# Five pairs of 512 tokens from the ninth unit on, two of their output tiles computed from g kept in the place of w_in, and attention ahead of them in even steps

## The chip, the cores and the metric

The program runs on one core of a Trainium2 chip. The metric is device time in microseconds (us) of one execution; lower is better. A core has these engines, each with an instruction stream of its own that runs in order: TensorE (PE in the profile; its weight loads are listed as PEld), VectorE (DVE), ScalarE (ACT), GpSimd (POOL) and SyncE (SP), which here issues nearly all DMA transfers. They wait for one another by semaphores. PE reads its operands from the on-chip memory SBUF and writes to the accumulators in PSUM.

## What is computed

Linear attention with positive random features (8 batches, 8 heads, 576 tokens, head dimension 64, 128 features), and behind it a layer of two matrix products on all 4608 tokens of 512 values:

```python
def phi(x):
    proj = np.einsum('bhsd,md->bhsm', x, omega)
    h = proj - np.sum(x * x, axis=-1, keepdims=True) / 2.0
    h = h - np.max(h, axis=-1, keepdims=True)
    return np.exp(h) / np.sqrt(m)
q_p, k_p = (phi(q_s), phi(k_s))
kv = np.einsum('bhsm,bhsd->bhmd', k_p, v)
num = np.einsum('bhsm,bhmd->bhsd', q_p, kv)
den = np.einsum('bhsm,bhm->bhs', q_p, np.sum(k_p, axis=2))[..., None] + 1e-06
x = num / den          # 4608 x 512 behind the transpose of the heads
h = x @ w_in           # 512 x 2048
g = h - np.tanh(h)
out = g @ w_out        # 2048 x 512
```

## The kernel before

**Precision.** Operands of the large products are split into a high and a low part in the type fp32r (`xh`, `xl`; `gh`, `gl`; two halves of each weight tile), and three products high*high, high*low, low*high are summed.

**Units and steps.** Tokens go through the second layer in units of 256 (`TC`), 18 in all, and its 2048 inner columns in 16 tiles `f` of 128. Units 0 and 1 run together, 512 columns wide, while the weights are still being decoded (`decode`, L435 to L451, from 1 MB tiles `raw` that DMA brings). From unit 2 on a unit has 8 steps `s`, each of two tiles f. In a step `ffn_h` (L468) makes 24 matmuls of 128x256 (2 f, 4 parts c of x's 512 values, 3 products) into one PSUM tile h, then ACT takes the tanh (L472), DVE subtracts it from h (L473), ACT casts to gh (L474) and DVE makes gl (L475). `ffn_out` (L486 to L488) adds the 12 products of the step before, 128x512 each, to the two output tiles `po0` and `po1` of the unit. A weight tile `wt[f]` holds, for both parts, 512 values of w_in and 512 of w_out.

**Attention.** Its work from batch 2 on and for units 3 to 17 runs between the steps, in generators: `k_unit(b, c)` for batch b and head pair c, `q_unit(ch, c)` for unit ch. There are four c to each. A q loads `qf`, splits it into `qx`, makes features, sums the denominator with `zb`, scales, transposes (`pt`), splits into `qh` and `ql`, multiplies with `kvw` (`pn`), adds two halves into `xs` (L397 to L400) and splits that into `xh` and `xl` (L406, L407). A table `start` says at which beat each generator begins; a step has two beats, and at each beat every living generator goes on to its next `yield`:

```python
for ch in range(3, NCH):
    for c in range(NC):
        k = 28 + 4 * c if ch == 3 else 42 + 4 * c if ch == 4 else 16 * (ch - 1) - 6 + 4 * c
        start.setdefault(k, []).append(("q", ch, c))
for b in range(2, B):
    for c in range(NC):
        k = 31 + 5 * c if b == 2 else 16 * (need[b] - 1) - 25 + 8 * c
```

Unit 2 begins at beat 32, unit ch at 16*ch. Ahead of the first step of a unit the loop runs generators on until the x of this unit is complete (`xdone`).

**Order.** A scheduler puts the instructions of each engine into their final order from the order of the code and from what they depend on; in the decoding phase loads keep the order of the code. Tiles with one tag share `bufs` buffers in turn, so a tile waits until the one that had its buffer is read. `xh` and `xl` hold two units, in turn by `ch % 2`. A unit's two output tiles are copied to SBUF (`o`, one buffer) and stored in the first step of the next unit.

## Time and profile before

| | before |
|---|---|
| three runs, us | 1069.51, 1071.07, 1070.82 (median 1070.82) |
| the profiled execution, us | 1070.01 |
| its span from first to last instruction, us | 1068.2 |
| mean granted clock of TensorE in it | 0.991 |
| instructions in the trace | 20318 |
| DMA packets and bytes | 35529, 55.91 MB |
| HBM read and written | 45.15 MB, 9.44 MB |

The profile is of one execution. "busy" is the time in which an engine has at least one instruction under way. The lines with 40 digits give the busy share of 40 equal slices of the span in tenths, and the clock line the share of full speed that TensorE was granted. A row of a group has its line in the program, engine, operation, written and read tiles, shape, count, then busy us and mean ns of one, then idle time ahead of it and what ended that. Matmuls overlap, so the time one takes up in a stream is the distance from its start to the next start and not its listed length.

### The profile page before, as it was taken

To read this page: it belongs to the slowest core of one execution; us is meant where nothing else is said; L and a number is where in the kernel's file an instruction comes from. 1 tells how busy PE (TensorE), PEld (TensorE's weight loads), DVE (VectorE), ACT (ScalarE), POOL (GpSimd) and SP (SyncE) were. 2 spreads that over 40 slices of the span, in tenths; PEclk is the share of its full clock that TensorE was granted. 3 is DMA by queue.
4 is the path that set the end of the run, shared out by engine and by line. 5 is a ranking of instruction groups with operands and counts; after the bars stand their busy time and mean duration, and the time that the engine had idled before them with its cause. 6 is when DMAs were issued, how large, how long until landed. Compare 5 with 4: busy or idle time off the path is not lost. (4 is left out here: it accounts for less than half of the span.)

```text
span 1068.2 us, 20318 instructions
## 1 busy us (share of the span) xinstructions
PE 1044.0 (98%) x6760; PEld 949.3 (89%) x6760; DVE 854.0 (80%) x3030; ACT 713.2 (67%) x1833; POOL 323.5 (30%) x553
## 2 busy tenths in 40 slices
PE   8988999989999999999999999999999999999998
...
DVE  6999985898888986788888888898888897666522
...
PEclk8999999998999999999999999999999999999999
DMA  8750401111111110011111111111101110000000
GB/s 266 234 212 12 178 4 48 43 43 38 33 53 33 53 33 31 11 53 33 52 34 52 34 28 53 33 48 29 51 22 52 29 41 11 30 11 26 1 21 20
DMA packets 35529, 55.91 MB, mean 52 GB/s; under 512 B 12256, under 2 KB 21600, under 8 KB 33376
## 3 DMA queue, kind: packets, MB, share of 16 engines
...
HBM read 45.15 MB, written 9.44 MB: 51 GB/s over the span
## 5 line engine op out<-in xcount | busy, mean ns | idle before, releaser
L468 PE MATMUL h<-xh,w 128*128 128x256 f32 (+1 forms) x2176 | 453.3, 292 | 3.8 <-DVE g L473 2.1
L468 PEld LDWEIGHTS h<-xh,w 128*128 128x128 f32 x2176 | 356.7, 191 | 14.1 <-DVE g L473 2.7
L468 PE MATMUL h<-xl,w 128*128 128x256 f32 (+1 forms) x1088 | 317.3, 292 | 0.5 <-DVE xl L407 0.5
L486 PE MATMUL po<-w,gh 128*128 128x512 f32 x544 | 214.2, 394 | 0.0
L468 PEld LDWEIGHTS h<-xl,w 128*128 128x128 f32 x1088 | 207.9, 191 | 6.7 <-DVE xl L407 0.8
L487 PE MATMUL po<-w,gh 128*128 128x512 f32 x544 | 213.7, 393 | 0.0
L488 PE MATMUL po<-w,gl 128*128 128x512 f32 x544 | 209.3, 391 | 0.0
L473 DVE TENSOR_TENSOR g<-h,g 128x512 f32<-128x512 f32 x144 | 98.8, 686 | 66.4 <-ACT g L472 65.3
L472 ACT ACTIVATE g<-h 128x512 f32<-128x512 f32 x144 | 85.1, 591 | 99.2 <-PE h L468 91.9
L474 ACT CAST gh<-g 128x512 fp32r<-128x512 f32 x144 | 89.4, 621 | 84.3 <-DVE g L473 82.7
L475 DVE TENSOR_TENSOR gl<-g,gh 128x512 fp32r<-128x512 f32 x144 | 109.9, 764 | 38.3 <-ACT gh L474 36.5
L488 PEld LDWEIGHTS po<-w,gl 128*128 128x128 f32 x544 | 102.2, 188 | 20.7
L486 PEld LDWEIGHTS po<-w,gh 128*128 128x128 f32 x544 | 102.5, 188 | 16.6
L487 PEld LDWEIGHTS po<-w,gh 128*128 128x128 f32 x544 | 102.5, 188 | 15.2
L347 DVE CUSTOM_DVE_ANT_0 junk<-phi_q,zb 128x128 f32<-128x128 f32 (+1 forms) x320 | 96.5, 303 | 14.7 <-ACT phi_q L150 0.5
L250 POOL TENSOR_TENSOR khl<-phi_ka,khl 128x256 fp32r<-128x256 f32 x48 | 38.0, 795 | 154.2 <-DVE khl L249 129.2
L150 ACT ACTIVATE phi_q<-phi_q,nb_q 128x128 f32<-128x128 f32 x240 | 79.0, 392 | 6.3 <-DVE nb_q L146 6.1
L258 POOL CAST vhl<-v 128x128 fp32r<-128x128 f32 (+1 forms) x144 | 45.7, 319 | 100.9 <-PE pk L266 82.4
L439 POOL TENSOR_SCALAR a<-a 128x1024 f32<-128x1024 f32 x14 | 59.0, 4214 | 54.7 <-ACT a L435 42.1
L387 DVE TENSOR_TENSOR ql<-pt,qh 128x512 fp32r<-128x512 f32 x60 | 41.1, 685 | 26.5 <-ACT qh L386 26.1
L259 DVE TENSOR_TENSOR vhl<-v,vhl 128x128 fp32r<-128x128 f32 (+1 forms) x144 | 45.2, 314 | 16.7 <-POOL vhl L258 13.0
L146 DVE CUSTOM_DVE_ANT_0 phi_q<-pj_q,phi_q 128x128 f32<-128x128 f32 x240 | 55.9, 283 | 1.1 <-ACT phi_q L143 1.0
...
## 6 DMA issues: line engine op xcount, KB each, us to landing
raw<-w SPq DMA_DIRECT2D x16, 1024.0 KB, 7.5
...
qf<-qT SPq DMA_DIRECT2D x72, 128.0 KB, 2.1
...
```

The source lines that it names most:

```text
L146: nc.vector.tensor_tensor_reduce(ph[:, j], pj[:, i, :M], ph[:, j], scale=-SCALE, scalar=3.0e38, op0=ALU.add, op1=ALU.min, accum_out=nb[:, ...
L150: nc.scalar.activation(ph[:, j], ph[:, j], AF.Exp, bias=nb[:, j : j + 1], scale=-1.0)
L347: nc.vector.tensor_tensor_reduce(bank("junk")[r], ph[r, i], kvs[b, c][1][r, h], scale=1.0, scalar=EPS, op0=ALU.mult, op1=ALU.add, accum_ou ...
L439: engine.tensor_scalar(a.bitcast(F32), a.bitcast(F32), 2.0**-15, 122879.9921875, op0=ALU.max, op1=ALU.min)
L468: nc.tensor.matmul(o, w_, x, start=i == 0, stop=i == len(prods) - 1)
L472: nc.scalar.activation(g, p, AF.Tanh)
L473: nc.vector.tensor_sub(g, p, g)
L474: nc.scalar.copy(gh, g)
L475: nc.vector.tensor_sub(gl, g, gh.bitcast(F32))
L486: nc.tensor.matmul(po[t], h, wt[f][:, 0, DM:], start=first, stop=False)
L487: nc.tensor.matmul(po[t], h, wt[f][:, 1, DM:], start=False, stop=False)
L488: nc.tensor.matmul(po[t], l, wt[f][:, 0, DM:], start=False, stop=last)
```

## The change

From unit 8 on, tokens go in five pairs of 512 (`NL`), each in 16 steps of one f. In a step `wide_h` makes 12 matmuls of 128x512 for h. The tokens 0 to 255 of a pair have their g split by ACT and DVE, 256 columns each, and `wide_out` adds its 6 products to `po0` and `po1` as before. The g of tokens 256 to 511 is split by POOL and written into the lower half of the place of w_in in `wt[f]`; behind the 16 steps the products of two more output tiles (`last`, 48 matmuls of 128x512 each) are made from it. As that place is overwritten, w_in is written to DRAM once it is decoded (`w_in_away`, 16 transfers of 512 KB) and brought back for each f of the later pairs into the upper halves of the places, 8 tiles f in a ring (`w_in_back`, 64 times four transfers of 128 KB).

A q unit now ends in a tile `later`, 512 tokens of x before the split, and the split into `xh` and `xl` is made per unit (`x_of`) or, for a pair, 512 wide (`next_x`), which for the next pair stands between the two last output tiles. Stores of units 0 to 7 use buffers of gl and gh. Output tiles, matmul shapes of attention, and units 0 to 7 are otherwise as they were. The beats at which attention starts are a new table: unit 2 still begins at 32, pair a begins at 128 + 40*a. The number of q and k units that start in each stretch of beats:

| beats | q, k before | q, k after |
|---|---|---|
| 28 to 31 | 1, 1 | 2, 1 |
| 32 to 47 | 5, 3 | 4, 3 |
| 48 to 63 | 4, 2 | 5, 3 |
| 64 to 79 | 4, 2 | 6, 1 |
| 80 to 95 | 4, 0 | 5, 2 |
| 96 to 111 | 4, 2 | 5, 2 |
| 112 to 127 | 4, 2 | 3, 2 |
| then, each 40 beats | 16 beats: 4, 2, at the end 4, 0 | 8, 4; 8, 4; 8, 2; 6, 0; 0, 0 |

```diff
...
+NQ = NT // TC
+C0 = 8
+NL = (NQ - C0) // 2
+NB = 8
...
-        tmp = att("tmp", [P, TC], F32, f"tmp_{n}")
-        xs = sb.tile([P, TC], F32, tag="xs", name=f"xs_{n}", bufs=2)
-        nc.scalar.copy(tmp[0:D], pn[D:P, 0])
-        nc.scalar.copy(tmp[D:P], pn[0:D, 1])
-        nc.vector.tensor_add(xs[0:D], pn[0:D, 0], tmp[0:D])
-        nc.vector.tensor_add(xs[D:P], pn[D:P, 1], tmp[D:P])
-        yield
-        x_split(ch, c, xs, nc.vector)
+        while ch > 3 and ch - 2 not in split:
+            yield
+        xs = later[:, c, ch % 2 * TC : ch % 2 * TC + TC]
+        nc.scalar.copy(xs[0:D], pn[D:P, 0])
+        nc.scalar.copy(xs[D:P], pn[0:D, 1])
+        nc.vector.tensor_add(xs[0:D], pn[0:D, 0], xs[0:D])
+        nc.vector.tensor_add(xs[D:P], pn[D:P, 1], xs[D:P])
         xdone[ch] = xdone.get(ch, 0) + 1
     def x_split(ch, c, x, engine):
-        nc.scalar.copy(xh[:, ch % 2, c], x)
-        engine.tensor_sub(xl[:, ch % 2, c], x, xh[:, ch % 2, c].bitcast(F32))
+        r = ch if isinstance(ch, slice) else ch % 2
+        nc.scalar.copy(xh[:, r, c], x)
+        engine.tensor_sub(xl[:, r, c], x, xh[:, r, c].bitcast(F32))
     wt = {}
...
     xh, xl = [sb.tile([P, 2, NC, TC], F32R, name=f"x{k}") for k in "hl"]
+    later = sb.tile([P, NC, 2 * TC], F32, name="later")
     def ffn_h(ch, s):
...
     def ffn_store(ch):
         for t, p in enumerate(pos[ch]):
-            if ch == NCH - 1 and t == 1:
-                o = sb.tile([P, DM], F32, tag="g", name=f"o_{ch}_{t}")
-                nc.vector.tensor_copy(o, p)
-            else:
-                o = sb.tile([P, DM], F32, tag="o", name=f"o_{ch}_{t}")
-                nc.scalar.copy(o, p)
-            r = ch * TC + t * P
-            nc.sync.dma_start(out[r : r + P, :], o)
+            store(p, ch * TC + t * P)
+    def store(p, r, engine=nc.scalar):
+        o = sb.tile([P, DM], F32, tag=bank("o"), name=f"o_{r}", bufs=1 if mode["o"][-1] == "g" else 2)
+        copy(engine, o, p)
+        nc.sync.dma_start(out[r : r + P, :], o)
+    w_dram = {}
+    def w_in_away(f):
+        w_dram[f] = tc.dram_tile([P, 2, DM], F32, name=f"w_in{f}")
+        nc.sync.dma_start(w_dram[f], wt[f][:, :, 0:DM].bitcast(F32))
+    def w_in_back(i):
+        f, k = i % NF, 2 * (i % NB)
+        for j in range(2):
+            for a in range(2):
+                nc.sync.dma_start(wt[k + j][:, a, TC:DM].bitcast(F32), w_dram[f][:, a, TC * j : TC * j + TC])
+    def w_in(a, f, i, c):
+        if a == 0:
+            return wt[f][:, i, c * P : (c + 1) * P]
+        j = TC + c % 2 * P
+        return wt[2 * (f % NB) + c // 2][:, i, j : j + P]
+    def wide_h(a, f):
+        p = ps.tile([P, 2, TC], F32, tag=bank("h"), name=f"h_w{a}_{f}")
+        prods = [(w_in(a, f, i, c), x[:, 0:2, c]) for c in range(NC)
+                 for i, x in ((0, xh), (0, xl), (1, xh))]
+        for i, (w_, x) in enumerate(prods):
+            nc.tensor.matmul(p, w_, x, start=i == 0, stop=i == len(prods) - 1)
+        g = sb.tile([P, 2, TC], F32, tag=bank("o"), name=f"g_w{a}_{f}", bufs=1 if mode["o"][-1] == "g" else 2)
+        e = sb.tile([P, 2, TC], F32R, tag="gh", name=f"ge_w{a}_{f}", bufs=2)
+        nc.scalar.activation(g, p, AF.Tanh)
+        nc.vector.tensor_sub(g, p, g)
+        nc.scalar.copy(e[:, 0], g[:, 0])
+        nc.vector.tensor_sub(e[:, 1], g[:, 0], e[:, 0].bitcast(F32))
+        hi, lo = [wt[f][:, i, 0:TC] for i in range(2)]
+        nc.gpsimd.tensor_copy(hi, g[:, 1])
+        nc.gpsimd.tensor_sub(lo, g[:, 1], hi.bitcast(F32))
+        return a, f, e[:, 0], e[:, 1]
+    def products(o, f, h, l):
+        nc.tensor.matmul(o, h, wt[f][:, 0, DM:], start=f == 0, stop=False)
+        nc.tensor.matmul(o, h, wt[f][:, 1, DM:], start=False, stop=False)
+        nc.tensor.matmul(o, l, wt[f][:, 0, DM:], start=False, stop=f == NF - 1)
+    def wide_out(a, f, h, l):
+        for t, p in enumerate(pos["w"]):
+            products(p, f, h[:, t * P : (t + 1) * P], l[:, t * P : (t + 1) * P])
...
-    x2 = {}
+    split = {2}
...
-        chain=True, kvw=(sb, 7), zb=(sb, 6), zb0=(a0, 4), phi=(a0, 8), ph5=(a0, 2), qf=(a0, 2), qt=(a0, 2),
+        chain=True, kvw=(sb, 6), zb=(sb, 6), zb0=(a0, 4), phi=(a0, 8), ph5=(a0, 2), qf=(a0, 2), qt=(a0, 2),
         kf=(a0, 3), native=True, junk=[junk, a0.tile([P, M], F32, name="junk1")],
-        norm=[nc.vector,nc.scalar], pj=["pj0", "pj1", "po0", "po1"], pk=["pk", "h0"],
+        norm=[nc.vector,nc.scalar], o=["gl", "gh"], pj=["pj0", "pj1", "po0", "po1"], pk=["pk", "h0"],
...
-        phi=(ak, 3), qh=(ak, 1), ql=(ak, 1), tmp=(ak, 1), kf=(ak, 1), kx=(ak, 1), qf=(ak, 2),
+        phi=(ak, 3), qh=(ak, 1), ql=(ak, 1), kf=(ak, 1), kx=(ak, 1), qf=(ak, 1),
...
+    def begins(a):
+        return 16 * C0 + 40 * a
+    for ch in range(3, NQ):
+        a, j = (ch - C0) // 2, (ch - C0) % 2 * NC
         for c in range(NC):
-            k = 28 + 4 * c if ch == 3 else 42 + 4 * c if ch == 4 else 16 * (ch - 1) - 6 + 4 * c
+            if ch < C0 + 2:
+                k = [(28,31,34,37),(42,45,48,52),(55,58,61,64),(67,70,73,76),(79,82,85,88),(91,94,97,100),(103,106,109,112)][ch - 3][c]
+            else:
+                k = begins(a - 1) + (-9 + 9 * (j + c) // 2 if a == 1 else -9 + 5 * (j + c))
             start.setdefault(k, []).append(("q", ch, c))
     for b in range(2, B):
+        a = ((b * S) // TC - C0) // 2
         for c in range(NC):
-            k = 31 + 5 * c if b == 2 else 16 * (need[b] - 1) - 25 + 8 * c
+            k = [28,50,80,112][b - 2] + [5,6,8,8][b - 2] * c if b < 2 + len([28,50,80,112]) else begins(a - 1) + -18 + 11 * c
             start.setdefault(k, []).append(("k", b, c))
     t = 32 - 2 * (NF - done)
-    assert min(start) >= t
+    assert min(start) >= t and all(k == int(k) for k in start)
     def beat():
         nonlocal t
...
     for s in range(done, NF):
         step(s, beat)
     for c in range(NC):
-        x_split(2, c, x2[c], nc.vector)
+        x_split(2, c, later[:, c, 0:TC], nc.vector)
     ffn_out(*prev)
     ffn_store(0)
     mode.update(pj=["pj0", "pj1"], pt=["pt"])
     prev = None
-    for ch in range(2, NCH):
+    def x_of(ch):
+        split.add(ch)
+        for c in range(NC):
+            x_split(ch, c, later[:, c, ch % 2 * TC : ch % 2 * TC + TC], nc.vector)
+    for ch in range(2, C0):
         out_tiles(ch)
+        while xdone[ch] < NC:
+            tick((), True)
+        if ch not in split:
+            x_of(ch)
         for s in range(NS):
-            while ch > 2 and xdone.get(ch, 0) < NC:
-                tick((), True)
+            if s > 0 and ch + 1 not in split and xdone.get(ch + 1) == NC:
+                x_of(ch + 1)
             g = (ch, s, *ffn_h(ch, s))
+            if ch == C0 - 1 and s == NS - 1 and xdone.get(C0 + 1) == NC:
+                x_of(C0 + 1)
             beat()
             if prev is not None:
                 ffn_out(*prev)
                 if s == 0:
                     ffn_store(ch - 1)
+            if ch == 2:
+                for f in range(2 * s, 2 * s + 2):
+                    w_in_away(f)
             beat()
             prev = g
     ffn_out(*prev)
-    ffn_store(NCH - 1)
+    ffn_store(C0 - 1)
+    mode.update(o=["g", "gl"])
+    def next_x(a):
+        pair = (C0 + 2 * a, C0 + 2 * a + 1)
+        for ch in pair:
+            while xdone.get(ch, 0) < NC:
+                tick((), True)
+        if split.isdisjoint(pair):
+            for c in range(NC):
+                x_split(slice(0, 2), c, later[:, c].rearrange("p (j t) -> p j t", j=2), nc.vector)
+            split.update(pair)
+        for ch in pair:
+            if ch not in split:
+                x_of(ch)
+    next_x(0)
+    for a in range(NL):
+        r = (C0 + 2 * a) * TC
+        out_tiles("w")
+        prev = None
+        for f in range(NF):
+            g = wide_h(a, f)
+            beat()
+            if prev is not None:
+                wide_out(*prev)
+            i = NF * a + f + 6
+            if NF <= i < NF * NL:
+                w_in_back(i)
+            beat()
+            prev = g
+        wide_out(*prev)
+        for i in range(2):
+            store(pos["w"][i], r + i * P)
+        for i in range(2):
+            p = ps.tile([P, DM], F32, tag=bank("h"), name=f"last_{a}_{i}")
+            for f in range(NF):
+                products(p, f, *[wt[f][:, j, i * P : (i + 1) * P] for j in range(2)])
+                if f % 4 == 3:
+                    beat()
+            store(p, r + (2 + i) * P, nc.vector if a == NL - 1 and i == 1 else nc.scalar)
+            if i == 0 and a < NL - 1:
+                next_x(a + 1)
```

**PE, a step of the last unit and of the last pair.** The names are h with unit (or w and pair) and step, w with f, po with the output tile. Before, the second half of a step's h and the first output products behind it:

```order
L468 MATMUL h_17_7_13949<-xh_100,w15_1615 128x256
L468 MATMUL h_17_7_13949<-xl_101,w15_1615 128x256
L468 MATMUL h_17_7_13949<-xh_100,w15_1615 128x256 x2
L468 MATMUL h_17_7_13949<-xl_101,w15_1615 128x256
L468 MATMUL h_17_7_13949<-xh_100,w15_1615 128x256 x2
L468 MATMUL h_17_7_13949<-xl_101,w15_1615 128x256
L468 MATMUL h_17_7_13949<-xh_100,w15_1615 128x256 x2
L468 MATMUL h_17_7_13949<-xl_101,w15_1615 128x256
L468 MATMUL h_17_7_13949<-xh_100,w15_1615 128x256
L486 MATMUL po0_17_13633<-w12_1479,gh_17_6_13931 128x512
L487 MATMUL po0_17_13633<-w12_1479,gh_17_6_13931 128x512
L488 MATMUL po0_17_13633<-w12_1479,gl_17_6_13932 128x512
```

Now, in step 14 of the last pair, with the six output products of step 12:

```order
L529 MATMUL h_w4_14_13097<-xh_100,w13_1523 128x512
L529 MATMUL h_w4_14_13097<-xl_101,w13_1523 128x512
L529 MATMUL h_w4_14_13097<-xh_100,w13_1523 128x512 x2
L542 MATMUL po0_w_12683<-w12_1477,ge_w4_12_13057 128x512
L543 MATMUL po0_w_12683<-w12_1477,ge_w4_12_13057 128x512
L544 MATMUL po0_w_12683<-w12_1477,ge_w4_12_13057 128x512
L542 MATMUL po1_w_12684<-w12_1477,ge_w4_12_13057 128x512
L543 MATMUL po1_w_12684<-w12_1477,ge_w4_12_13057 128x512
L544 MATMUL po1_w_12684<-w12_1477,ge_w4_12_13057 128x512
L529 MATMUL h_w4_14_13097<-xl_101,w13_1523 128x512
L529 MATMUL h_w4_14_13097<-xh_100,w13_1523 128x512
```

Where 12 matmuls of 256 columns (the first 9 rows) made one f for 256 tokens, 12 of 512 columns now make it for 512 tokens, and the 6 output products of a step stand inside the h of a later one.

**PE, where unit 3 begins.** The last row of each piece is the first matmul that reads the fourth part (c = 3) of unit 3's x. Before, attention's matmuls of k (batch 2, third head pair) and of the q's of unit 4 stand in front of it:

```order
L394 MATMUL pn_3_3_2634<-ql_3_3_2588,kvw_1_3_996 128x256
L142 MATMUL pj_kb2_2_2_2683<-om_89,kx_2_2_2410 128x256 x2
L266 MATMUL pk_2_2_2448<-khl_2_2_0_2515,vhl_2_2_0_2516 128x256 x2
L266 MATMUL pk_2_2_2448<-khl_2_2_2_2521,vhl_2_2_2_2522 128x256 x2
L363 MATMUL pt_4_0_2695<-ident_64,phi_q4_0_2530 128x128 x4
L142 MATMUL pj_q4_1_0_2782<-om_89,qx_4_1_2704 128x256 x2
L142 MATMUL pj_q4_1_2_2788<-om_89,qx_4_1_2704 128x256 x2
L266 MATMUL pk_2_2_2448<-khl_2_2_4_2645,vhl_2_2_4_2646 128x256 x2
L468 MATMUL h_3_0_2716<-xh_100,w0_219 128x256
```

Now:

```order
L269 MATMUL pk_2_2_2394<-khl_2_2_0_2440,vhl_2_2_0_2441 128x256 x2
L269 MATMUL pk_2_2_2394<-khl_2_2_2_2446,vhl_2_2_2_2447 128x256 x2
L468 MATMUL h_3_1_2953<-xl_101,w2_448 128x256
L468 MATMUL h_3_1_2953<-xh_100,w2_448 128x256 x2
L468 MATMUL h_3_1_2953<-xl_101,w2_448 128x256
L468 MATMUL h_3_1_2953<-xh_100,w2_448 128x256 x2
L468 MATMUL h_3_1_2953<-xl_101,w2_448 128x256
L468 MATMUL h_3_1_2953<-xh_100,w2_448 128x256
L145 MATMUL pj_q4_0_2_2633<-om_89,qx_4_0_2556 128x256 x2
L468 MATMUL h_3_0_2853<-xh_100,w0_220 128x256
```

Matmuls of h of unit 3's second step now stand there, with less of attention among them.

**SP, in the first 30 us.** Names are raw with f, qf with unit and c, kf and v with their buffers. Before:

```order
L81 DMA raw3_340<-w 128x1024
L81 DMA qf_1_0_368<-qT 128x256
L81 DMA qf_0_1_370<-qT 128x256
L81 DMA kf_1_0_432<-kT 128x576
L81 DMA v1_125<-va 128x9x64
```

Now:

```order
L84 DMA raw3_341<-w 128x1024
L84 DMA qf_1_0_369<-qT 128x256
L509 DMA w_in0_1882<-w0_220 256x1x512
L84 DMA qf_0_1_371<-qT 128x256
L84 DMA kf_1_0_433<-kT 128x576
L84 DMA v1_126<-va 128x9x64
```

The transfer of the first w_in to DRAM, which waits for the decoding of tile 0, stands ahead of the loads of a q, a k and a v.

9 lines of the change are left out of this document (1 added, 8 removed).

## The prediction

> **What bounds the kernel now.** I read the page first, then PE's waits, then single matmul starts in the timeline. The page says that TensorE (PE) is never idle for long, and that VectorE (DVE) comes second:
>
> ```profile
> PE 1044.0 (98%) x6760; PEld 949.3 (89%) x6760; DVE 854.0 (80%) x3030; ACT 713.2 (67%) x1833; POOL 323.5 (30%) x553
> PE   8988999989999999999999999999999999999998
> DVE  6999985898888986788888888898888897666522
> PEclk8999999998999999999999999999999999999999
> DMA  8750401111111110011111111111101110000000
> ```
>
> Three things stand in the slices (26.7 us each): DVE is nearly full where the weights are decoded (slices 2 to 5), with DMA busy too; the granted clock dips in the tenth slice; DVE has little left to do in the last three. From slice 11 on PE is the bound, so time is gained by making its instruction stream shorter and by closing its gaps. The largest gap behind the start is the one at 236 to 250 us, in the windows (us, PE busy, PEld, DVE, ACT, POOL, granted clock, DMA share, GB/s) and in PE's waits from 200 to 270 us:
>
> ```profile
> 230.00:235.00 5.00, 5.00 (x34) 4.49 (x33) 4.68 (x24) 3.65 (x11) 1.26 (x3) 1.00 0.00 0
> 235.00:240.00 5.00, 2.18 (x18) 1.98 (x17) 4.33 (x17) 2.96 (x10) 1.88 (x3) 1.00 0.23 79
> 240.00:245.00 5.00, 3.28 (x15) 2.46 (x14) 4.32 (x17) 4.91 (x13) 1.99 (x7) 0.57 0.14 52
> 245.00:250.00 5.00, 4.47 (x21) 4.18 (x21) 4.92 (x15) 2.71 (x9) 3.52 (x6) 0.50 0.47 121
> 250.00:255.00 5.00, 5.00 (x41) 5.00 (x40) 4.54 (x20) 3.96 (x12) 1.72 (x4) 0.90 0.09 26
> ...
> PE pj_kb L142 <- DVE nb_km L146: 2.8, 1, 2.8
> PE pt L363 <- DVE xs L400: 1.1, 1, 1.1
> ```
>
> Idle time is 5.00-2.18, 5.00-3.28 and 5.00-4.47, 5.1 us together; behind it the granted clock is 0.57, 0.50 and 0.90, which costs 0.43x3.28 + 0.5x4.47 + 0.1x5 = 4.1 us more. So this one place loses **9.2 us**. It is where unit 2 ends and the first matmuls of unit 3 wait for the last x of unit 3.
>
> **The matmuls.** Single starts in the timeline (start us, length us), first in unit 0/1, where everything is 512 columns wide, then a step of the last unit, 24 matmuls of 256 columns and 12 of 512:
>
> ```profile
> 111.79 0.39 PE L468 MATMUL h<-xh,w 128*128 128x512 f32 x1
> 117.23 0.39 PE L468 MATMUL h<-xh,w 128*128 128x512 f32 x1
> ...
> 1011.01 0.28 PE L468 MATMUL h<-xh,w 128*128 128x256 f32 x1
> 1013.89 0.40 PE L486 MATMUL po<-w,gh 128*128 128x512 f32 x1
> 1016.64 0.28 PE L468 MATMUL h<-xh,w 128*128 128x256 f32 x1
> ```
>
> From 111.79 to 117.23 there are 24 matmuls of 512: 0.2267 us each. From 1011.01 to 1013.89, 24 of 256: 0.120 each, so 512 columns in two halves cost 0.240. The change makes 1920 such matmuls (10 units x 8 steps x 24) into 960 of 512, and leaves the 960 output products as they are. Counting h alone, 80 x (2.88 - 12x0.2267) = 12.8 us. Counting whole steps, 5.63 now against 24x0.2267 = 5.44 in the pairs, 80 x 0.19 = 15.2 us, since the mixing of widths goes too; but attention's narrow matmuls stay strewn among them, so part of that stays. I take **-13**, ends -11 and -15.
>
> [...]
>
> **The gap of unit 3.** DVE's own pace in it:
>
> ```profile
> 229.14 0.68 DVE L473 TENSOR_TENSOR g<-h,g 128x512 f32<-128x512 f32 x1
> 245.78 0.43 DVE L407 TENSOR_TENSOR xl<-xs,xh 128x256 fp32r<-128x256 f32 x1
> ```
>
> The first is the last g of unit 2, the second the last x of unit 3. In DVE's order they lie 54 rows apart before and 28 after, because the q's of unit 3 start at beats 28, 31, 34, 37 instead of 28, 32, 36, 40. At 16.6 us for 54 rows, 28 rows take 8.6 us; h of unit 2 ends some 1.3 us ahead of its g. PE has, by its order, from the end of that h to the first matmul that needs this x about 10.6 us of work (24 output products, 19 h, the rest attention's). So the wait should nearly go, and the slow clock with it: **-7**, ends 0 and -9.2.
>
> **What the even steps ask of DVE.** Two stretches price attention: windows, then g, ql (one for each q) and kvs (one for each k) of each:
>
> ```profile
> 534.00:600.00 66.00, 66.00 (x458) 61.46 (x457) 56.66 (x219) 47.64 (x130) 25.13 (x51) 1.00 0.13 37
> 667.00:734.00 67.00, 67.00 (x459) 62.10 (x459) 60.89 (x240) 49.48 (x135) 23.15 (x46) 1.00 0.12 37
> 934.00:1000.00 66.00, 66.00 (x441) 60.77 (x440) 43.42 (x165) 37.19 (x94) 0.00 (x0) 1.00 0.05 15
> ...
> L473 DVE TENSOR_TENSOR g<-h,g x9: 675/681/692, 538.8 to 595.0; 128x512 f32<-128x512 f32 x9
> L387 DVE TENSOR_TENSOR ql<-pt,qh x5: 677/681/692, 535.9 to 591.8; 128x512 fp32r<-128x512 f32 x5
> L308 DVE TENSOR_TENSOR kvs<-pk,kvs x2: 285/288/291, 557.5 to 588.4; 128x128 f32<-128x128 f32 x2
> ...
> L473 DVE TENSOR_TENSOR g<-h,g x10: 690/692/693, 939.6 to 996.0; 128x512 f32<-128x512 f32 x10
> L387 DVE TENSOR_TENSOR ql<-pt,qh x5: 690/692/692, 943.4 to 993.9; 128x512 fp32r<-128x512 f32 x5
> ```
>
> With 1.38 us of DVE in a step (g and gl at 0.69), the last stretch gives (43.42 - 13.8)/5 = 5.9 us for a q; the first then gives (56.66 - 12.4 - 29.5)/2 = 7.4 for a k. Before, a unit of 16 beats starts 4 q and 2 k as a rule: 23.6 + 14.8 + 11 = 49 us in about 56. After, units 2 to 6 start 4+3, 5+3, 6+1, 5+2 and 5+2, together 25 q and 11 k: 147.5 + 81.4 + 55.2 = 284 us. PE's 66 us from 534 to 600 hold 9.4 steps of 5.63, so 13 us of attention with 5 q and 2 k; five units of 45 + 13 to 15 are some 294 us, and DVE is at 0.97 in them. At 0.91 (667 to 734) PE lost nothing. The ends are 0, since work may slide into unit 7, which starts only 3 q, and, if DVE runs 3% short over the five, +9; I take **+4**. In a pair (40 beats) it is 8 q, 4 k and 16 steps of 0.69 + 0.45: 95 us in 2x56 - 16x0.19 = 109, which is 0.87, as now.
>
> **POOL, DMA and the pair boundaries.** Rows by line for what is added or moved, and DMA's:
>
> ```profile
> L472 ACT ACTIVATE g<-h 128x512 f32<-128x512 f32 x144 | 85.1, 591 | 99.2 <-PE h L468 91.9
> L474 ACT CAST gh<-g 128x512 fp32r<-128x512 f32 x144 | 89.4, 621 | 84.3 <-DVE g L473 82.7
> L406 ACT CAST xh<-xs 128x256 fp32r<-128x256 f32 x60 | 24.5, 409 | 20.5 <-DVE xs L400 20.2
> L475 DVE TENSOR_TENSOR gl<-g,gh 128x512 fp32r<-128x512 f32 x144 | 109.9, 764 | 38.3 <-ACT gh L474 36.5
> L407 DVE TENSOR_TENSOR xl<-xs,xh 128x256 fp32r<-128x256 f32 x60 | 27.1, 452 | 1.9 <-ACT xh L406 1.3
> L250 POOL TENSOR_TENSOR khl<-phi_ka,khl 128x256 fp32r<-128x256 f32 x48 | 38.0, 795 | 154.2 <-DVE khl L249 129.2
> L258 POOL CAST vhl<-v 128x128 fp32r<-128x128 f32 x96 | 33.0, 346 | 98.4 <-PE pk L266 82.4 <-DVE w L451 7.2 <-DMA v<-vt 3.5
> ...
> qf<-qT SPq DMA_DIRECT2D x72, 128.0 KB, 2.1
> raw<-w SPq DMA_DIRECT2D x16, 1024.0 KB, 7.5
> 100.00:115.00 15.00, 15.00 (x72) 12.20 (x71) 13.58 (x17) 11.20 (x15) 8.34 (x2) 1.00 0.63 252
> L451 DVE SCALAR_TENSOR_TENSOR w<-m,a x16: 1203/1216/1251, 22.2 to 156.1; 128x1024 fp32r<-128x1024 uint32 x16
> ```
>
> ACT and DVE give half of cast and subtraction (0.62 - 0.41, 0.76 - 0.45) to POOL, which does 80 times a cast of 256 (between 0.35 and 0.8) and a subtraction (0.8): at most 1.6 us in a step of 5 to 7 us. Nothing waits for it before the last two tiles, which come behind all 16 steps, except the g buffer two steps later. Cost: 0. In a pair PE leaves less cover for e: 6 products and 12 h, 4.1 us, against 0.59 + 0.69 + 0.41 + 0.45 = 2.1 us of chain; before it was 5.6 against 2.7.
>
> Each step fetches 4 x 128 KB, issued up to 8 steps ahead; such a load lands in 2.1 us. At 252 GB/s PE ran 72 matmuls in 15 us, so traffic does not slow it. A fetch waits for PE on SP's queue, and q, k and v loads queue behind it, as they now queue behind waits for DVE; their lead is a beat or more: 0 taken. The 16 transfers out are tied to decoding, from 23.4 (22.2 + 1.2) to 157.3 us, and stand on SP's queue ahead of startup loads, each 512 KB, half a raw load's. In slices 1 to 3 DMA and DVE are the tight ones: three fall there, at most (7.5 - 2.1)/2 = 2.7 us each by the two DMA rows, mostly under DVE's backlog: **+0.5**, ends 0 and +8. At each of four pair boundaries 4 casts and subtractions of 512 (0.62 + 0.76) follow the last q's under 48 products (11 us): **+1** in all, ends 0 and +6. The tail keeps one copy and one store: 0.
>
> **Sum** for the profiled execution, 1070.0 us (span 1068.2): 1070.0 - 13 - 7 + 4 + 0.5 + 1 = **1055.5**. The median of the three runs is 0.8 above it.
>
> **The rivals.**
>
> (1) All covered: -15 and -9, nothing new: 1046. For: DVE's load is spread more evenly and before lost 0 at 0.91. Against: 0.97 stands in no long stretch of the trace.
>
> (2) DVE becomes the bound in units 2 to 6, and the gap of unit 3 only moves: 1070 - 13 - 1 + 8 + 1 = 1065. For: the sum of 0.97, and that unit 2 of before, with 5 q and 3 k, lost PE time.
>
> (3) What makes narrow matmuls dear comes with the step, not with each of them, so that wide ones take 0.24 here and the change does not do what it says: 1070 - 7 + 5.5 = 1068.5. Against: 24 wide ones in a row at 0.2267.
>
> (4) Slower: POOL takes DVE's time in the pairs. The mechanism shows in gl, which reads two SBUF tiles; first with POOL idle, then with POOL at work:
>
> ```profile
> L475 DVE TENSOR_TENSOR gl<-g,gh x10: 691/692/693, 1010.0 to 1061.1; 128x512 fp32r<-128x512 f32 x10
> L475 DVE TENSOR_TENSOR gl<-g,gh x93: 676/693/1264, 252.5 to 896.2; 128x512 fp32r<-128x512 f32 x93
> ```
>
> A blocked gl loses up to 0.57 us. The change adds 32 POOL instructions to a pair, all reading SBUF. If each costs DVE more than (109 - 95)/32 = 0.44 us, DVE passes 109 us; at 0.6 it is short by 5 us in each of three pairs, and with the half clock behind each wait 10: 1070 - 13 - 7 + 5.5 + 30 = 1085. It decides the sign from 14.5 us of such waits on. Against: the median of 693, so most gl are not blocked. [...]
>
> (5) SP's queue holds q or k loads back behind fetches that wait for PE: a late q costs a step, 5 us, at each of four boundaries: 1070 - 13 - 7 + 5.5 + 20 = 1075.
>
> **How the numbers follow.** Forecast (1050 to 1060) 0.55, (1) 0.12, (2) 0.15, (3) 0.05, (4) 0.08, (5) 0.05. The range leaves out (4), (5) and the far end of (2): 1046 to 1066. About 0.2% is what a measurement of this kernel can tell from no change, so faster means below 1068. Faster is the forecast, (1) and (2): 0.82. Within 0.2% is (3), and 0.04 from the near ends of (4) and (5): 0.09; the rest of these two is slower: 0.09.
>
> **What would show it.** In the pairs, 512-wide h at 0.227 us from start to start, not 0.23 to 0.24. Between units 2 and 3, no window with a granted clock of 0.5 and PE's wait below 2 us. In units 2 to 6, DVE above 0.93 and PE's windows full; a PE wait on DVE there is rival 2. gl or ge far above its median in the pairs, with PE waiting on DVE, is rival 4. PE waiting for a DMA of w, or ACT for qf, is rival 5. I am wrong on the sign if the pairs hold more than 15 us of PE waits.

## The result, and the profile after

| | before | the change |
|---|---|---|
| median, us | 1070.94 | 1079.71 |
| lowest to highest, 4 runs each, us | 1069.51 to 1071.07 | 1078.36 to 1080.17 |
| ratio to before, 95% interval | | 1.0081 [1.0069, 1.0093] |
| profiled execution and its span, us | 1070.01, 1068.2 | 1079.91, 1078.1 |

The change makes the kernel slower by 0.8%. The same lines of the page as were shown of before, now of the changed kernel:

```profile
PE 1045.1 (97%) x5800; PEld 898.3 (83%) x5800; DVE 857.6 (80%) x3014; ACT 698.5 (65%) x1817; POOL 423.9 (39%) x713
...
PE   8988999999999999999999999999999999999998
DVE  6999986889989999999998988989798958742220
PEclk9999999999999999999999999999999999999999
DMA  8953631111111101111123213443243314332301
```

POOL has 100 us more to do, DVE is at 0.9 or more in 20 slices (8 before) and has less left at the end; PE's row looks full and does not show what was lost. So I measure PE by starts: the time from one matmul's start to the next, less the median for that width (512 columns 227 ns, 256 columns 120, and so on down to 109 for 128), summed over a stretch. This is called **lost** below. The medians alone add up to 1009.7 us before and 997.2 after: PE has **12.5 us** less to do.

| lost by PE, us | 0 to 100 | 100 to 230 | 230 to 255 | 255 to 535 (units 3 to 7) | 535 to the end |
|---|---|---|---|---|---|
| before | 40.9 | 0.6 | 9.7 | 0.5 | 2.0 |
| the change | 41.7 | 0.7 | 4.5 | 10.7 | 18.3 |

The gap of unit 3 is half gone (-5.2); 10.2 us are new in the units, 16.3 in the pairs. The sum, -12.5 + 0.8 + 0.1 - 5.2 + 10.2 + 16.3 = +9.7, comes near the 9.9 us between the spans.

The windows (us, PE busy, PEld, DVE, ACT, POOL, granted clock, DMA share, GB/s), first of the kernel before, then of the changed one for the gap, the units and the first four of the five pairs:

```profile
255.00:535.00 280.00, 280.00 (x1906) 259.13 (x1905) 233.86 (x913) 194.46 (x520) 85.57 (x163) 1.00 0.13 37
```

```profile
235.00:240.00 5.00, 4.06 (x29) 3.47 (x27) 3.90 (x12) 4.87 (x14) 3.72 (x9) 1.00 0.02 3
240.00:245.00 5.00, 3.97 (x18) 3.63 (x19) 4.67 (x22) 2.31 (x7) 3.33 (x6) 0.68 0.30 71
255.00:535.00 280.00, 275.40 (x1865) 251.72 (x1864) 258.40 (x1020) 211.04 (x569) 100.39 (x194) 1.00 0.14 40
538.00:661.00 123.00, 118.91 (x609) 98.28 (x608) 108.77 (x415) 82.02 (x226) 63.01 (x115) 1.00 0.25 75
661.00:777.00 116.00, 114.07 (x593) 95.41 (x592) 101.74 (x386) 80.45 (x224) 63.03 (x115) 1.00 0.37 112
777.00:890.00 113.00, 111.05 (x568) 92.53 (x567) 92.03 (x357) 72.05 (x196) 46.63 (x86) 1.00 0.33 102
890.00:987.00 97.00, 97.00 (x468) 81.28 (x467) 56.05 (x199) 46.34 (x116) 20.16 (x32) 1.00 0.34 105
```

In units 3 to 7 DVE goes from 0.84 (233.86/280) to 0.92, and PE, which was never idle there, has gaps. The pairs lose time only while attention goes on beside them: of their 18.3 us, 17.7 lie between 538 and 890 us, and from 890 to 987 PE is busy for 97.00 of 97.00 us. PE's waits of the changed kernel from 250 to 1000 us (what waited, for what, us in total, times, longest) are short and of many kinds, most of them for DVE:

```profile
PE h_w L529 <- DVE g_w L533: 2.7, 4, 1.4
PE pj_q L145 <- DVE qx L132: 2.2, 4, 1.2
PE pk L269 <- POOL khl L253: 2.0, 5, 0.9
PE pk L305 <- DVE c L302: 1.4, 2, 1.0
PE po_w L544 <- DVE ge_w L535: 1.0, 4, 0.4
```

### The profile page after: what moved, and what is told of

It reads as the page before. It is cut to its first block, busy times and chain, and to the rows that moved or that the text cites. A ratio compares the mean times of both kernels' runs of the same rounds, so it can differ in the third digit from the quotient of the medians.

```text
span 1078.1 us, 19335 instructions
## 1 busy us (share of the span) xinstructions
PE 1045.1 (97%) x5800; PEld 898.3 (83%) x5800; DVE 857.6 (80%) x3014; ACT 698.5 (65%) x1817; POOL 423.9 (39%) x713
## 4 chain that ended last, share of the span: by engine, by line
PE 68%; DVE 23%; ACT 4%; issue 3%; DMA 1%; POOL 1%; DVEq 0%; POOLq 0%; ACTq 0%; SPq 0%
PE h_w L529 15%; PE h L468 13%; DVE junk L350 4%; PE po L488 4%; PE po L487 4%; PE po L486 4%; PE last L544 3%; PE last L542 3%; PE last L543 3%; PE po_w L544 2%; PE po_w L542 2%; PE po_w L543 2%; PE pk L269 2%; PE pj_q L145 2%; PE pt L366 2%
## 5 line engine op out<-in xcount | busy, mean ns | idle before, releaser
L529 PE MATMUL h_w<-xh,w 128*128 128x512 f32 x640 | 210.2, 393 | 2.7 <-DVE g_w L533 2.7
L468 PE MATMUL h<-xh,w 128*128 128x256 f32 (+1 forms) x896 | 200.5, 301 | 4.2 <-DVE g L473 2.1
L468 PEld LDWEIGHTS h<-xh,w 128*128 128x128 f32 x896 | 150.5, 191 | 12.7 <-DVE g L473 2.8
L529 PEld LDWEIGHTS h_w<-xh,w 128*128 128x128 f32 x640 | 118.9, 188 | 26.0 <-DVE g_w L533 4.4
L468 PE MATMUL h<-xl,w 128*128 128x256 f32 (+1 forms) x448 | 134.9, 302 | 0.0
L529 PE MATMUL h_w<-xl,w 128*128 128x512 f32 x320 | 125.4, 392 | 0.0
L468 PEld LDWEIGHTS h<-xl,w 128*128 128x128 f32 x448 | 85.8, 192 | 4.1 <-DVE xl L405 0.2
L486 PE MATMUL po<-w,gh 128*128 128x512 f32 x224 | 88.6, 396 | 0.0
L487 PE MATMUL po<-w,gh 128*128 128x512 f32 x224 | 88.2, 394 | 0.0
L488 PE MATMUL po<-w,gl 128*128 128x512 f32 x224 | 85.2, 394 | 0.0
L529 PEld LDWEIGHTS h_w<-xl,w 128*128 128x128 f32 x320 | 60.2, 188 | 10.8
L538 POOL TENSOR_TENSOR w<-g_w,w 128x256 fp32r<-128x256 f32 x80 | 67.2, 841 | 4.2
```

The lines of the kernel that those rows point to most:

```text
L468: nc.tensor.matmul(o, w_, x, start=i == 0, stop=i == len(prods) - 1)
L486: nc.tensor.matmul(po[t], h, wt[f][:, 0, DM:], start=first, stop=False)
L487: nc.tensor.matmul(po[t], h, wt[f][:, 1, DM:], start=False, stop=False)
L488: nc.tensor.matmul(po[t], l, wt[f][:, 0, DM:], start=False, stop=last)
L529: nc.tensor.matmul(p, w_, x, start=i == 0, stop=i == len(prods) - 1)
L538: nc.gpsimd.tensor_sub(lo, g[:, 1], hi.bitcast(F32))
```

## The experiments

Theory A: POOL's added work in the pairs lengthens DVE's operations. Theory B: the new table of starts packs more attention into a beat than DVE can do. Rivals come with each run. All results in one table; ratios are to the kernel before on the same chip, where it had medians of 1070.12 to 1070.90 us. What was lost is from the profiled execution of each run, which for e8 took 1072.41 us, 2.9 above its median.

| run | median, us | ratio [95%] | lost 230-255 | 255-535 | 535-end |
|---|---|---|---|---|---|
| e1 no POOL split | 1069.97 | 0.9998 [0.9988, 1.0007] | 4.5 | 10.9 | 8.1 |
| e2 no w_in transfers | 1079.56 | 1.0082 [1.0065, 1.0098] | 4.5 | 11.0 | 17.6 |
| e3 units, new table | 1075.08 | 1.0044 [1.0029, 1.0059] | 4.1 | 10.9 | 2.0 |
| e4 units, old table | 1063.46 | 0.9935 [0.9920, 0.9950] | 0.3 | 2.2 | 2.0 |
| e5 = e4 + POOL work | 1074.42 | 1.0034 [1.0021, 1.0047] | 0.3 | 2.1 | 13.2 |
| e6 a scaling to ACT | 1072.53 | 1.0018 [1.0009, 1.0027] | 3.7 | 10.5 | 11.6 |
| e7 split on ACT, DVE | 1076.44 | 1.0054 [1.0038, 1.0070] | 4.6 | 11.1 | 14.3 |
| e8 two pairs | 1069.52 | 0.9989 [0.9978, 1.0000] | 0.2 | 9.2 | 8.8 |
| e9 = e4, a beat later | 1063.61 | 0.9937 [0.9919, 0.9954] | 1.6 | 1.3 | 2.2 |
| e10 = e4, uneven | 1062.58 | 0.9926 [0.9908, 0.9943] | 0.3 | 3.0 | 1.4 |
| e13 POOL's cast only | 1069.67 | 0.9992 [0.9983, 1.0002] | 4.4 | 10.8 | 7.8 |
| e14 = e3, even beats | 1075.21 | 1.0042 [1.0026, 1.0058] | 1.4 | 12.2 | 0.9 |
| e15 = e3, less DVE | 1071.22 | 1.0007 [0.9998, 1.0016] | 1.3 | 11.0 | 0.9 |
| e16 = e3, less ACT | 1075.94 | 1.0052 [1.0035, 1.0069] | 4.6 | 10.8 | 1.6 |
| e18 = e3, least DVE | 1066.73 | 0.9970 [0.9958, 0.9982] | 1.6 | 6.3 | 0.9 |
| e17 one pair | 1070.29 | 1.0000 [0.9990, 1.0009] | 0.3 | 2.0 | 11.6 |
| e19 one pair, earlier | 1070.54 | 1.0002 [0.9991, 1.0013] | 0.2 | 2.1 | 11.7 |

### What each part of the change costs

**No POOL split** (e1). In `wide_h`:

```diff
-        nc.gpsimd.tensor_copy(hi, g[:, 1])
-        nc.gpsimd.tensor_sub(lo, g[:, 1], hi.bitcast(F32))
```

> Left out: POOL's two operations of each step of the pairs (the cast and the subtraction that put the second half of g where w_in was), so the two last output tiles of a pair are made from what was there. Theory A (POOL's 80 casts and 80 subtractions, 102 us in all, lie over DVE's operations that read two SBUF tiles and lengthen them, and DVE comes late for PE): the 16 us more that PE loses in the pairs than in the same units of before fall to below 5, junk and vhl come back to 0.30 and 0.31 us, and the time is 1064 to 1069 us. Theory B (the new table of starts puts more attention into a beat than DVE can do, with or without POOL): the time PE loses in the pairs stays above 12 us, the time is 1075 or more. Theory C (the w_in transfers disturb PE or the loads of q and k): no change, 1078 to 1081. The lost time in units 2 to 7 (10.9 us) stays by all three.

**No w_in transfers** (e2):

```diff
-                for f in range(2 * s, 2 * s + 2):
-                    w_in_away(f)
...
-            if NF <= i < NF * NL:
-                w_in_back(i)
```

> Left out: w_in is neither written to DRAM nor fetched back, so pairs 1 to 4 multiply x by what stands in its place. Theory C (the 16 writes of 512 KB and 256 fetches of 128 KB cost PE time, by the SP queue or by their traffic): at least 5 us less, 1075 or less. Theories A and B: within 2 us of 1079.7.

**Units alone, new table** (e3): `C0 = 18` and no code of the pairs; units from 10 and batches from 6 start as before.

```diff
-C0 = 8
+C0 = 18
...
-            if ch < C0 + 2:
+            if ch < 10:
...
-                k = begins(a - 1) + (-9 + 9 * (j + c) // 2 if a == 1 else -9 + 5 * (j + c))
+                k = 16 * (ch - 1) - 6 + 4 * c
```

> No pairs: the change's code with units of 256 to the end, its x tile, its one q buffer, its table of starts for units 3 to 9 and batches 2 to 5, the table of before behind them, no w_in transfers. Theory B (the new table itself): PE loses 8 to 11 us in units 2 to 7 as with the change, only 4 to 5 us at the gap between units 2 and 3, and the time is 1072 to 1078. Theory A (only the pairs' POOL work costs): PE loses below 2 us in units 2 to 7, and the time is 1063 to 1068, since half of the gap is gone. Theory C: as A.

**Units alone, old table** (e4): the same with the two formulas of the kernel before.

```diff
+            k = 28 + 4 * c if ch == 3 else 42 + 4 * c if ch == 4 else 16 * (ch - 1) - 6 + 4 * c
...
+            k = 31 + 5 * c if b == 2 else 16 * (need[b] - 1) - 25 + 8 * c
```

> As the run with units alone, with the table of before all through, so that only the x tile, the split of x by units and the single q buffer differ from the kernel before. If these cost nothing: 1069 to 1073, the gap of 9 to 10 us between units 2 and 3 as before, below 2 us lost in units 2 to 7. If the single x tile or the single q buffer is what makes PE wait in units 2 to 7 (theory D): 5 us or more lost there with the table of before too, and 1075 or more.

The four runs take the change apart. Without the table and the pairs it is 6.7 us faster than before (1063.46 against 1070.16 on the same chip); the table costs 11.6 (e3 less e4); the pairs bring 5.1 (e1 less e3) as long as POOL does not split g; POOL's split costs 9.7 (the change less e1). -6.7 + 11.6 - 5.1 + 9.7 = +9.5. The transfers cost nothing that shows (1079.56 without them, 1079.71 with them): theory C is out. Two expectations were missed: neither case of e4 had the gap closing with the old table, and in e1 the pairs still lose 6 us more than the units did, where theory A had below 5, and its time is 1 us above A's range. In e4 the window of the gap has no idle time at all, and PE no wait in it:

```profile
230.00:255.00 25.00, 25.00 (x177) 23.20 (x176) 23.39 (x97) 20.89 (x59) 11.80 (x23) 1.00 0.19 57
255.00:535.00 280.00, 279.39 (x1897) 258.11 (x1896) 235.42 (x915) 194.70 (x522) 87.22 (x169) 1.00 0.12 37
```

So the gap is closed by what e4 shares with the change (the tile `later`, the split of x by whole units, or other and fewer buffers, those of the stores among them; which of them wasn't tried), and the new table opens half of it again.

### How POOL costs PE

DVE's operations in the first three pairs (line, operation, shapes, count, busy us and mean ns, idle before), first of the change, then without the POOL split:

```profile
L350 DVE CUSTOM_DVE_ANT_0 junk<-phi_q,zb 128x128 f32<-128x128 f32 (+1 forms) x116 | 41.8, 360 | 5.9 <-ACT phi_q L153 1.1
L535 DVE TENSOR_TENSOR ge_w<-g_w,ge_w 128x256 fp32r<-128x256 f32 x48 | 27.7, 578 | 3.7 <-ACT ge_w L534 3.2
L132 DVE TENSOR_TENSOR qx<-qf,qx 64x256 fp32r<-64x256 f32 x26 | 13.4, 515 | 0.8
L533 DVE TENSOR_TENSOR g_w<-h_w,g_w 128x512 f32<-128x512 f32 x48 | 32.8, 683 | 3.5 <-ACT g_w L532 3.2
```

```profile
L350 DVE CUSTOM_DVE_ANT_0 junk<-phi_q,zb 128x128 f32<-128x128 f32 (+1 forms) x114 | 36.5, 320 | 6.3 <-ACT phi_q L153 1.2
L535 DVE TENSOR_TENSOR ge_w<-g_w,ge_w 128x256 fp32r<-128x256 f32 x48 | 23.8, 496 | 4.0 <-ACT ge_w L534 3.4
L132 DVE TENSOR_TENSOR qx<-qf,qx 64x256 fp32r<-64x256 f32 x26 | 12.3, 473 | 0.8
L533 DVE TENSOR_TENSOR g_w<-h_w,g_w 128x512 f32<-128x512 f32 x48 | 32.8, 684 | 4.4 <-ACT g_w L532 4.2
```

The first three read two tiles in SBUF and take longer beside POOL's split (360 against 320, 578 against 496 and 515 against 473 ns); g_w, which reads one of its two from PSUM, does not (683 against 684 ns). Next stands DVE in all, by windows of the change and of e1 that hold the same work (1156 and 1153 DVE instructions):

```profile
538.00:890.00 352.00, 344.02 (x1766) 286.23 (x1765) 302.54 (x1156) 234.51 (x645) 172.67 (x316) 1.00 0.32 96
```

```profile
538.00:880.00 342.00, 339.78 (x1766) 286.34 (x1765) 286.70 (x1153) 235.42 (x645) 111.90 (x220) 1.00 0.33 99
```

The same operations take DVE 15.8 us longer while POOL splits g. PE's waits in these windows, of the change, then of e1:

```profile
PE h_w L529 <- DVE g_w L533: 2.7, 4, 1.4
PE pj_q L145 <- DVE qx L132: 1.5, 2, 1.2
PE po_w L544 <- DVE ge_w L535: 1.0, 4, 0.4
...
PE pk L269 <- POOL khl L253: 0.8, 2, 0.5
```

```profile
PE pk L269 <- POOL khl L253: 0.2, 1, 0.2
PE h_w L529 <- DVE g_w L533: 0.2, 1, 0.2
PE pj_q L145 <- DVE qx L132: 0.2, 1, 0.2
```

So most of what POOL's split adds to them ends with DVE, and a small part with POOL's own khl.

**POOL's work put into units of 256** (e5), in `ffn_h` of e4:

```diff
+        if ch >= 8:
+            nc.gpsimd.tensor_copy(g[:, 0], g[:, 1])
+            nc.gpsimd.tensor_sub(g[:, 0], g[:, 1], g[:, 0])
```

> The run with units alone and the table of before (1063.5 us), with the pairs' POOL work added and nothing else of the pairs: from unit 8 on, each of the 80 steps has POOL cast 256 elements of g and subtract them, into a half of g that nobody reads any more. Theory A (POOL's work lengthens DVE's operations on SBUF by lying over them, whatever the shape of the units): junk goes from 0.304 to above 0.33 us, qx from 0.43 to above 0.46, DVE's busy time grows by 10 to 20 us, and the time by 2 to 9 us. Rival A2 (the gain of leaving POOL's work out came from somewhere else in the pairs: POOL's queue ahead of khl, or the last tiles waiting for what POOL wrote): DVE's durations stay within 3 per cent and the time within 1.5 us.

The time rises by 11.0 us, all of it behind 535 us. DVE, for 1236 and 1238 instructions, takes 17.9 us more, and junk goes from 296 to 355 ns in these windows (of e4, then of e5):

```profile
535.00:900.00 365.00, 364.39 (x2502) 337.73 (x2501) 314.50 (x1236) 257.70 (x695) 129.88 (x247) 1.00 0.13 38
L350 DVE CUSTOM_DVE_ANT_0 junk<-phi_q,zb 128x128 f32<-128x128 f32 (+1 forms) x120 | 35.5, 296 | 5.5 <-ACT zb L313 0.4 <-ACT phi_q L153 0.3
```

```profile
535.00:911.00 376.00, 370.56 (x2499) 338.71 (x2498) 332.37 (x1238) 260.35 (x698) 187.14 (x351) 1.00 0.13 37
L350 DVE CUSTOM_DVE_ANT_0 junk<-phi_q,zb 128x128 f32<-128x128 f32 (+1 forms) x120 | 42.6, 355 | 4.0
```

Theory A holds, outside the pairs too, and its price is above its range; of the operations named, the two of qx grew from 419 and 421 to 461 and 443 ns. A2 falls as the whole cause. As a part of it it isn't excluded: in e5 PE waits 1.0 us for khl from POOL's queue (0.2 in e4), and ACT 7.4 us for POOL to be done with the buffer of g.

**POOL's cast only** (e13):

```diff
-        nc.gpsimd.tensor_sub(lo, g[:, 1], hi.bitcast(F32))
```

> The changed kernel with POOL's cast in the pairs but without its subtraction (left out, so the low half that the last tiles read is old): 80 casts of 0.43 us stay of 102 us of POOL work. Theory A by time: a third of the 9.7 us stays, about 1073. If only POOL's operation with two inputs stands in DVE's way: 1070 to 1071. If each POOL operation costs the same whatever its length: 1075.

DVE in the first three pairs of this run:

```profile
L350 DVE CUSTOM_DVE_ANT_0 junk<-phi_q,zb 128x128 f32<-128x128 f32 (+1 forms) x116 | 37.1, 320 | 6.3 <-ACT phi_q L153 0.6 <-ACT zb L313 0.4
L535 DVE TENSOR_TENSOR ge_w<-g_w,ge_w 128x256 fp32r<-128x256 f32 x48 | 26.2, 547 | 4.8 <-ACT ge_w L534 4.3
```

1069.67 is the time without any POOL work (1069.97), so the cost comes with the subtraction, 80 of 0.84 us with two inputs; it is nearest the second case. junk is back at 320; ge_w, which runs right beside the cast, is not (547 against 496), but PE did not wait for that. Whether it is the subtraction's second input or its length, this run can't tell; both operations read SBUF.

**Split on ACT and DVE** (e7):

```diff
-        nc.gpsimd.tensor_copy(hi, g[:, 1])
-        nc.gpsimd.tensor_sub(lo, g[:, 1], hi.bitcast(F32))
+        nc.scalar.copy(hi, g[:, 1])
+        nc.vector.tensor_sub(lo, g[:, 1], hi.bitcast(F32))
```

> The changed kernel with the pairs' split of the second half of g on ACT (cast) and DVE (subtraction) in the place of POOL: ACT gets 80 operations of about 0.41 us, DVE 80 of about 0.45, 36 us, while the 18 us by which POOL's work lengthened DVE's own go. Theory A (only DVE's total counts): DVE is 10 to 20 us busier, PE loses as much in the pairs as with POOL or some us more, 1078 to 1086. If POOL costs more than DVE's lengthened operations show (its slowness ahead of the last tiles, its queue): below 1076.

It falls between the two cases. For the same work DVE is busier than with POOL (305.98 us from 538 to 885 us for 1765 matmuls, against 302.54 from 538 to 890 us for 1766), yet PE loses 4 us less in the pairs (14.3 against 18.3): here POOL costs more than the time by which DVE's operations grow. What the rest is stays open.

### Why the new table costs PE

**One of DVE's scalings to ACT** (e6), in the changed kernel:

```diff
-        chain=False, native=False, norm=[nc.vector, nc.vector, nc.vector, nc.scalar], junk=[junk],
+        chain=False, native=False, norm=[nc.vector, nc.scalar, nc.vector, nc.scalar], junk=[junk],
```

> The changed kernel with two of each four scalings of phi_q on ACT in the place of one: 60 operations of 0.31 us leave DVE (18.5 us), 60 of 0.40 us come to ACT (24 us). If DVE's work is what PE waits for (theory B in the units, A in the pairs): of the 10.9 us that PE loses in units 2 to 7 some 4 to 7 go, of the 18 us in the pairs 3 to 6, and the time is 1068 to 1073 us. If it is the length of the chains from engine to engine, which ACT makes longer here: no gain, 1078 or more.

The total is as expected, but all of the gain lies in the pairs (18.3 to 11.6), and none in units 3 to 7 (10.5 for 10.7). So taking this much work off DVE did not help in the units, which theory B, as put here, had expected.

**Two pairs from unit 14** (e8), heads every 3.5 beats from unit 5 on:

```diff
-C0 = 8
+C0 = 14
...
+        return 58 + (7 * (4 * (ch - 5) + c)) // 2
...
+            k = 31 + 5 * c if b == 2 else q_at(need[b], 0) - 19 + 7 * c
```

> Two pairs only, from unit 14 on; the attention ahead of them spread over units 0 to 13 at 3.5 beats a head (the table of before: 4; the change: 3.1), correct in all parts. Theory B (the denser beat is the cost in the units): PE loses below 3 us in units 2 to 13, two pairs bring 2.4 us each against the 1063.5 us of units alone, and lose up to 4 us to POOL in the first: 1059 to 1063. If taking x one unit further ahead costs at any beat: 1066 or more.

A miss: 3.5 beats cost too, 9.2 us from 255 to 535 us, with DVE at 0.90 (250.6/280). Its time is that of the second case, that taking x further ahead costs at any beat, which no run separates from the closer starts. The miss led to theory F, that the place of a start within a step counts, which three runs tried: **every start a beat later** (e9, old table), **heads at 0, 5, 8, 13** (e10, old table) and **all heads on even beats** (e14, new table). The first two are shown against e4, the third against e3:

```diff
-            k = 28 + 4 * c if ch == 3 else 42 + 4 * c if ch == 4 else 16 * (ch - 1) - 6 + 4 * c
+            k = 28 + 4 * c if ch == 3 else 43 + 4 * c if ch == 4 else 16 * (ch - 1) - 5 + 4 * c
...
-            k = 31 + 5 * c if b == 2 else 16 * (need[b] - 1) - 25 + 8 * c
+            k = 31 + 5 * c if b == 2 else 16 * (need[b] - 1) - 24 + 8 * c
```

```diff
-            k = 28 + 4 * c if ch == 3 else 42 + 4 * c if ch == 4 else 16 * (ch - 1) - 6 + 4 * c
+            k = 28 + 4 * c if ch == 3 else 42 + 4 * c if ch == 4 else 16 * (ch - 1) - 6 + (0, 5, 8, 13)[c]
```

```diff
-                k = [(28,31,34,37),(42,45,48,52),(55,58,61,64),(67,70,73,76),(79,82,85,88),(91,94,97,100),(103,106,109,112)][ch - 3][c]
+                k = [(28,32,34,38),(42,46,48,52),(54,58,60,64),(66,70,72,76),(78,82,84,88),(90,94,96,100),(102,106,108,112)][ch - 3][c]
```

> The run with units alone and the table of before (1063.5 us), with every start from unit 4 and batch 3 on one beat later, so that heads begin behind a step's out in the place of behind its h; as dense as before. Theory F (the place within the step counts: which FFN operations an attention operation stands behind on the in-order engines): PE loses 10 us or more behind 255 us in the place of 4.2, 1069 or more. Theory B (only the density of starts counts): the loss stays below 6 us, 1062 to 1066.

> The run with units alone and the table of before, with the heads of a unit from 5 on at 0, 5, 8 and 13 beats in the place of 0, 4, 8 and 12: as many a unit, but the second and fourth on odd beats and at uneven distances. Theory F: PE loses 8 us or more behind 255 us in the place of 4.2, 1067 or more. Theory B (mean density): below 6 us, 1062 to 1066.

> The run with units alone and the new table (1075.1 us), with the heads of units 3 to 9 moved by one beat where they stood on an odd one, so that all begin on even beats, as many in as many beats. Theory F: the 10.9 us lost between 255 and 535 us fall to 5 or below, 1069 or less. Theory B: 9 us or more are still lost there, 1073 to 1077.

F falls in all three: from 255 to 535 us only 1.3 and 3.0 us are lost at the old density, wherever heads start, and 12.2 at the new one.

**Less DVE work** (e15), **less ACT work** (e16), **least DVE work** (e18), all on e3, in the loop of the scalings; e16 skips ACT's, e18 has `i < 3`:

```diff
             e = bank("norm")
+            if i == 0 and not native:
+                continue
```

> The run with units alone and the new table (1075.1 us), with one of DVE's three scalings of phi_q left out for every head from unit 3 on (so a quarter of phi_q isn't divided by its sum): 60 operations of 0.31 us, 18.5 us, leave DVE and nothing comes to ACT. If DVE's work in the dense beats is what PE waits for: of the 10.9 us lost between 255 and 535 us 5 or more go, 1065 to 1070. If it is the length of the chains or ACT: at most 2 go, 1073 or more.

> The same kernel with ACT's one scaling of phi_q left out for every head from unit 3 on, and DVE's three kept: 24 us leave ACT. If ACT's work in the dense beats is what counts: 5 us or more of the 10.9 go, 1065 to 1070. If DVE's: at most 3 go, 1072 or more.

> The run with units alone and the new table (1075.1 us), with all three of DVE's scalings of phi_q left out for every head from unit 3 on: 180 operations of 0.31 us, 55 us, leave DVE, nothing comes to ACT, and DVE's share between 255 and 535 us should go from 0.92 to about 0.84, that of the table of before. If a full DVE is what PE waits for in the dense beats: below 4 of the 10.9 us stay, and with the gap between units 2 and 3 the time is 1060 to 1066. If it is the length of the chains or the few buffers that hold them: 8 us or more stay, 1068 or more.

DVE from 255 to 535 us, of e3, e15 and e18:

```profile
255.00:535.00 280.00, 275.23 (x1856) 250.99 (x1856) 258.30 (x1018) 210.67 (x567) 99.52 (x192) 1.00 0.14 41
```

```profile
255.00:535.00 280.00, 275.55 (x1862) 251.11 (x1861) 255.22 (x994) 210.62 (x573) 100.56 (x200) 1.00 0.14 40
```

```profile
255.00:535.00 280.00, 277.64 (x1896) 255.20 (x1895) 249.40 (x965) 213.85 (x582) 104.02 (x202) 1.00 0.14 40
```

ACT's scaling is out: 24 us less of it change nothing for the better (1075.94 against 1075.08). DVE's work counts: 55 us less give 8.4 of the 11.6 us. But e15 and e18 fall between their two cases. DVE's share in the window barely fell, 0.92, 0.91, 0.89, and PE lost 10.9, 11.0, 6.3 there; the gain of e15 lay at the gap and behind.

DVE's share does not tell what PE loses. In e9, with the old distances between starts, a later stretch of 280 us has DVE at 0.90, as e8 has from 255 to 535 us:

```profile
575.00:855.00 280.00, 279.34 (x1918) 258.56 (x1917) 253.04 (x963) 204.69 (x547) 100.11 (x197) 1.00 0.14 40
```

PE loses 1.6 us there, against 9.2 in e8. Nor do short full stretches tell it. Of the stretches of 8 us that begin at each us from 255 to 535 us, DVE is above 0.95 in 11% before, 16% in e4, 17% in e18 and 34% in e3. But e4 and e18 lose 2.2 and 6.3 us, and in e3 PE loses 0.39 us in such a stretch and 0.29 in the others. So the new table costs PE time, and part of that goes when DVE has less to do. What the rest is stays open: starts closer together, x finished further ahead, and the few buffers that hold a head's tiles for longer come with the table at once, and no run separates them.

### A version that beats both

e4 does, at 0.9935 [0.9920, 0.9950] of before; e9 and e10 are as fast. **One pair** (e17, `C0 = 16` and the old table but for units 16 and 17) and **one pair in time** (e19, the second and third pieces in the place of the first) were to add 2.4 us:

```diff
...
+            if ch > 15:
+                k = 234 + 12 * (ch - 16) + 3 * c
...
+            if ch in (15, 16, 17):
+                k = {15: (218, 222, 226, 230), 16: (232, 234, 237, 239), 17: (241, 243, 245, 247)}[ch][c]
...
+            if b == 7:
+                k = (199, 207, 215, 223)[c]
```

> The version that the runs point to: units of 256 to unit 15 with the change's x tile and the table of before, and one pair for units 16 and 17, when all attention is done, so that POOL's work in it meets none of DVE's and nothing has to be fetched back; only the heads of units 16 and 17 start closer, 3 beats apart. A fifth of the 12 us that five pairs saved on PE, 2.4 us, from the 1063.5 of units alone: 1060 to 1063. If the closer heads of the last two units cost as the new table did: 1063 to 1065.

> The version with one pair once more, with the heads of units 16 and 17 early enough that the pair finds its x done (the run before waited 9 us for them at the pair's start, three waits of PE for later and xh): 2.4 us from the 1063.5 of units alone, less what closer heads cost there: 1060 to 1063. If the wait comes back in another place: 1064 or more.

Both missed, with the same 9 us lost at the pair's start. PE's waits of e19 from 850 to 1060 us:

```profile
PE pt L366 <- DVE later L399: 3.8, 2, 1.9
PE h_w L529 <- ACT xh L404: 2.2, 1, 2.2
PE h_w L529 <- DVE g_w L533: 0.6, 1, 0.6
```

The last heads run one behind the other, each waiting for the one buffer `pt` in PSUM to be read, and none of the second layer's matmuls stand between them: `next_x` runs the heads to their end before the pair begins. Starting them earlier, closer to one another, did not mend that.

## Why the prediction was wrong

1. **The matmuls, -13: right.** 12.5 us by the medians of start to start. In the last pair, 18 matmuls of a step:

```profile
1000.28 0.39 PE L529 MATMUL h_w<-xl,w 128*128 128x512 f32 x1
...
1004.36 0.39 PE L529 MATMUL h_w<-xl,w 128*128 128x512 f32 x1
```

   4.08 us, 0.2267 each. Rival 3 is out.

2. **The gap, -7: size near, reason wrong.** It gave 5.2, but not through the earlier starts of unit 3: with the old starts it closes wholly (e4), and the new ones leave 4.1 (e3). The 28 rows in the place of 54 in DVE's order hold what the table and the new tile did together, and were put down to the table.

3. **DVE in units 2 to 6, +4, ends 0 and +9: mis-sized, and the first step that failed.** It is 10.2; the table as a whole, with its part of the gap, costs 11.6 (e3 less e4). The failing step is "At 0.91 (667 to 734) PE lost nothing" with "if DVE runs 3% short over the five": it prices PE's loss by DVE's sum against the time, and treats DVE as free until that sum is too long. DVE came out at 0.92 in units 3 to 7, where 0.97 was worked out for units 2 to 6, so by this step PE should have lost nothing. Rival 2 named DVE, but it too has DVE short of time, which in the sum it never was. What the runs show in its place is a cost of the table itself: with DVE at 0.89 and 0.90 PE loses 6.3 and 9.2 us with closer starts (e18, e8), and 1.6 at 0.90 with the old ones (e9), and 55 us less of DVE's work take 4.6 of the 10.9 us in this window away (e18). By which waits the closer starts cost the rest stays open.

4. **POOL, "Cost: 0": the dearest of the steps that failed.** Without POOL's split the change is level with before (1069.97 against 1070.16). Rival 4 was right in kind, at 0.08: 9.7 us (e1), against the 30 it was priced at. Two readings failed. gl was the only witness, with a median of 693, while junk, ge_w and qx grow by 12, 17 and 9% here. And the threshold of 0.44 us for each POOL instruction came from a pair's mean ("0.87, as now"): the 15.8 us over three pairs are 0.16 for each of the 96, well below it, and still PE lost 10.2 us by it. As in point 3, DVE had time to spare in the sum (302.54 us of 352), and PE waited for single results of it. What the trace of before shows beside that median was given too little: of those 93 gl 30 took 737 to 1264 ns, each of them beside a POOL instruction, and the others at most 711. In e1 and e5 it is again operations with two SBUF inputs that are longer with POOL's work than without (junk 360 against 320 ns, and 355 against 296), while g_w, with one input in SBUF, did not grow (683 against 684). In e13 one of these operations, ge_w, still grows beside the cast, which reads SBUF as well (547 against 496), but the time shows no cost of it (1069.67 against 1069.97).

5. **Boundaries, +1, ends 0 and +6:** above the upper end. The pairs without POOL's split lose 8.1 where the units lost 2.0, of it 6.0 between 538 and 659 us, in the first pair, so it is no cost of each boundary. What the first pair's share is made of was not taken apart.

6. **Transfers, +0.5: right;** 0 by e2, and rival 5 is out. The tail, 0: right.

By starts, the misses add up: the time rose by 9.7 us where -14.5 was forecast. Of these 24.2 us, POOL's split makes 10.2, the units 6.2, the pairs without it 5.1, the gap 1.8, the matmuls 0.5 and what was lost ahead of the gap 0.4.

"I am wrong on the sign if the pairs hold more than 15 us of PE waits" is what came by starts: 18.3. By the profile's idle time, by which the prediction read waits, it is 8.0 (538 to 890 us).
